# A weight conversion's low-word step moved behind its high-word step, and one accumulator closed by column halves

## The chip, the cores and the metric

The kernel runs on one core of a Trainium2 chip. The metric is the device time of one execution in microseconds (us), lower being better. TensorE (PE in the profile) multiplies matrices into PSUM, VectorE (DVE) and ScalarE (ACT) work element by element, GpSimd (POOL) does small jobs, and SyncE (SP) issues most of the DMA transfers. Each engine works through its own queue of instructions in the order in which they were built, and waits on semaphores for the others.

## The reference

Two computations follow each other. A retention block (batch 4, 8 heads, 768 positions, head width 64) keeps a decaying state per head, and its output becomes a 3072 x 512 matrix x. A feed-forward block then computes `silu(x @ w_in) @ w_out`, with 512 features in and out and 2048 in between:

```
state = gamma * state + outer(k[t], v[t]);   y[t] = scale * q[t] @ state
h = x @ w_in;   g = h / (1 + exp(-h));   out = g @ w_out
```

The five inputs are q, k, v in float32 and the two weight matrices in float64; the output is float32. The kernel receives a float64 weight as two 32-bit words, a low and a high one.

## The kernel before, in words

**Tiling.** The 768 positions are cut into six chunks c of 128, and with the four batches b that makes 24 units of attention. The inner width of 2048 is cut into 16 slices f of 128. For each chunk, x is a block of 512 columns (four batches of 128 positions).

**First stage.** For every pair (c, f) a group of twelve 128x512 matmuls (`multiply`, L682) makes h: eight into the accumulator `ha`, four into `hb`, because each operand is split into a high and a low part to keep float32 accuracy. There are 96 groups. `close_steps` then ends a group: ACT copies `ha` out of PSUM (L692), DVE subtracts `hb` (L697), ACT applies silu (L702), and SP stores the result g to DRAM (L708). The accumulators come from `turn`, which hands out three PSUM banks in rotation, so that the `hb` of a group takes the bank that the `ha` of the group before it had. The attention units are woven between the groups by `visit`.

**Weight conversion.** `load_w` loads a weight slice i (0 to 15 are w_in, 16 to 31 are w_out) as a tile `wf` of 128 x 1024 words into one of two buffers. `convert_steps` turns it into float32: ACT takes the absolute value of the high word (L204, tile `ca`), DVE takes the sign (L207), ACT converts the low word (L210; for w_out in place in `wf`, for w_in into `cw`), DVE clamps, shifts and combines (L212, L216), and DVE adds the low part (L222). A converted w_out slice is stored to DRAM (`wod`) and read back later.

**What sets the order.** PE's order is written by hand. On the other engines it is written by hand up to about the first tenth of the run (`early_order`, ended at L914); after that a scheduler in the build places each instruction by its own estimate of when its inputs are there. `queue(ins)` puts what is built inside it behind the instruction `ins` on that engine's queue; while the order is written by hand (`written`), it does nothing. The high-word step L204 stands inside such a block, the low-word step L210 in none.

**Second stage.** For every chunk, `oa` and `ob` accumulate `g @ w_out` for four batches over 16 slices (L1023). In the last chunk the last two slices are done batch by batch (L1031), first `ob`, then `oa`, so that the batches close one after the other. Each block then goes through ACT (copy `ob`, L1044), DVE (combine with `oa`, L1049) and SP (store, L1052); for the last batch DVE and the store work in two halves of 256 columns.

Of the kernel before, what the change touches and what calls it, by code (L numbers as in the profile page):

```python
# [13 lines left out]
FP32 = mybir.dt.float32  # L14
# [3 lines left out]
AF = mybir.ActivationFunctionType  # L18
# [15 lines left out]
def kernel(  # L34
# [28 lines left out]
    nc = tc.nc  # L63
    B, H, S, D = q.shape
    DM, DF = moe_w_in.shape
    C = 128
# [3 lines left out]
    NF = DF // 128  # L70
# [5 lines left out]
    scale = 1.0 / math.sqrt(D)  # L76
# [24 lines left out]
    def bits(x):  # L101
        return float(np.array(x, np.uint32).view(np.float32))
# [89 lines left out]
    def convert_steps(i, out):  # L192

        t = staged.pop(i)
        if not wide:
            out.append(t)
            return
        words = t.rearrange("p (c w) -> p c w", w=2)
        lo, hi = words[:, :, 0], words[:, :, 1]
        a = conv.tile([128, DM], U32, tag="ca", name=f"ca_{i}")  # L200
        s = conv.tile([128, DM], U32, tag="cs", name=f"cs_{i}")
        r = lo if i >= NF else conv.tile([128, DM], U32, tag="cw", name=f"cw_{i}")
        with queue(evac[0] if evac else None):
            nc.scalar.activation(out=a.bitcast(FP32), in_=hi.bitcast(FP32), func=AF.Abs,  # L204
                                 scale=2.0 ** -3)
        yield
        nc.vector.tensor_scalar(out=s, in0=hi, scalar1=0x80000000, scalar2=None,  # L207
                                op0=ALU.bitwise_and)
        yield
        nc.scalar.activation(out=r.bitcast(FP32), in_=lo, func=AF.Copy, scale=2.0 ** -27,  # L210
                             bias=2.0 ** 25)
        nc.vector.tensor_scalar(out=a.bitcast(FP32), in0=a.bitcast(FP32),  # L212
                                scalar1=bits(872 << 20), scalar2=bits((1127 << 20) - 1),
                                op0=ALU.max, op1=ALU.min)
        yield
        nc.vector.scalar_tensor_tensor(out=s, in0=a, scalar=3, in1=s,  # L216
                                       op0=ALU.logical_shift_left, op1=ALU.bitwise_xor)
        yield
        yield
        yield  # L220
        w = s if i < NF else conv.tile([128, DM], U32, tag="cw", name=f"cw_{i}")
        nc.vector.tensor_tensor(out=w, in0=s, in1=r, op=ALU.add)  # L222
        out.append(w.bitcast(FP32))

    def convert_w(i):

        if patient[0]:
            waiting.append(i + W_AHEAD)
        elif i + W_AHEAD not in staged:
            load_w(i + W_AHEAD)  # L230
        out = []
        steps = convert_steps(i, out)
        for _ in range(6):
            next(steps, None)

        def rounded():
            list(steps)
            return out[0]

        return rounded  # L240

    def early_slice(i):

        out = []
        yield from convert_steps(i, out)
        yield
        steps = split_steps(i, out[0], "wi", scale, w_sb, None)
        next(steps)
        yield from steps
# [4 lines left out]
    def queue(ins):  # L254

        return ExitStack() if written[0] or ins is None else tc.issue_after(ins)
# [69 lines left out]
    for j in range(2):  # L326
        for a in range(HP):
            nc.scalar.activation(out=decay[:, j, a, :], in_=lag[:, :D], func=AF.Exp,
                                 scale=float(lg[2 * a + j]))
# [10 lines left out]
    for h in range(H):  # L340
        nc.scalar.activation(out=gk[:, 0, h : h + 1], in_=pos, func=AF.Exp,
                             scale=float(-lg[h]))
# [27 lines left out]
    def banks(tag, name, n=2):  # L370
        return ps_u.tile([128, n, 512], FP32, tag=tag, name=name)
# [3 lines left out]
    def turn(name):  # L375
        turns[0] += 1
        return ps_h.tile([128, 512], FP32, tag=f"h{turns[0] % 3}", name=name)
# [334 lines left out]
    got, ready, wo, w_got = {}, {}, {}, {}  # L712
# [19 lines left out]
    def w_out(f):  # L732
        list(split_w(f, w_got.pop(f), "wo", 1.0, wo))
        get_w(f + W_READ)
# [3 lines left out]
    def split(n):  # L738
        if n >= len(order):
            return  # L740
        c, f = order[n]
        get(n + G_AHEAD)
        g = got.pop(n)
        if f % 4 == 0:
            blocks[n // 4] = xpool.tile([128, 3, 4, NT], FP32R, tag="xt", name=f"gs_{c}_{f}")
        t = blocks[n // 4][:, :, f % 4, :]
        nc.scalar.activation(out=t[:, 0, :], in_=g, func=AF.Copy, scale=HALF)  # L747
        high = t[:, 0, :].bitcast(FP32)
        nc.vector.tensor_tensor(out=t[:, 1, :], in0=g, in1=high, op=ALU.subtract)  # L749
        nc.vector.scalar_tensor_tensor(out=t[:, 2, :], in0=t[:, 1, :].bitcast(FP32),  # L750
                                       scalar=-1.0 / EPS, in1=high,
                                       op0=ALU.mult, op1=ALU.add)
        ready[n] = t
# [196 lines left out]
    parts = {first_far: FAR}  # L950
# [50 lines left out]
    for c in range(NC):  # L1001
        acc = []
        for b in range(B):
            if b < 2:
                u = banks("sy"[b], f"o{b}_{c}")
                acc.append([u[:, i] for i in range(2)])
            else:
                acc.append([turn(f"oa{b}_{c}"), turn(f"ob{b}_{c}") if b == 2 else
                            banks("q", f"ob{b}_{c}", 1)[:, 0]])
        early_f = NF if c < NC - 1 else NF - 2  # L1010
        for f in range(NF):
            n = c * NF + f
            split(n + S_AHEAD)
            if n < 4:
                w_out(NF - 4 + n)
            t = ready[n]
            if f >= early_f:
                continue
            for b in range(B):
                gh, glo, gm = (t[:, i, ts(b, C)] for i in range(3))  # L1020
                oa, ob = acc[b]
                for o, g, i in (oa, gh, 0), (oa, glo, 1), (ob, gm, 2):
                    nc.tensor.matmul(o, lhsT=g, rhs=wo[f][:, i, :], start=f == 0 and i != 1,  # L1023
                                     stop=f == NF - 1 and i != 0)

        for b in range(B if early_f < NF else 0):
            oa, ob = acc[b]
            for o, parts in (ob, (2,)), (oa, (0, 1)):
                for f in range(early_f, NF):
                    for i in parts:  # L1030
                        nc.tensor.matmul(o, lhsT=ready[c * NF + f][:, i, ts(b, C)],  # L1031
                                         rhs=wo[f][:, i, :], start=False,
                                         stop=f == NF - 1 and i != 0)
        for b in range(B):
            oa, ob = acc[b]
            o = one.tile([128, DM], FP32, tag=("kt", "qt")[b % 2], name=f"o_{c}_{b}",
                         bufs=(2, 3)[b % 2])
            rows = ds(b * S + c * C, C)
            if c < NC - 1:
                nc.scalar.activation(out=o, in_=oa, func=AF.Copy, scale=ONE_E)  # L1040
                nc.vector.tensor_tensor(out=o, in0=o, in1=ob, op=ALU.subtract)  # L1041
                nc.scalar.dma_start(out=out[rows, :], in_=o)
                continue
            nc.scalar.copy(out=o, in_=ob)  # L1044

            n = 2 if b == B - 1 else 1
            for i in range(n):
                cols = ts(i, DM // n)
                nc.vector.scalar_tensor_tensor(out=o[:, cols], in0=oa[:, cols], scalar=ONE_E,  # L1049
                                               in1=o[:, cols], op0=ALU.mult,  # L1050
                                               op1=ALU.subtract)
                nc.sync.dma_start(out=out[rows, cols], in_=o[:, cols])  # L1052
# [30 lines left out]
```

## Time and profile before

| what | us |
|---|---|
| three runs | 625.62, 621.43, 625.50 |
| median | 625.50 |
| the profiled execution, its own time | 627.48 |
| its span, first to last instruction | 625.70 |
| PE matmul busy | 602.2 |
| DVE busy | 393.4 |
| ACT busy | 332.5 |

The profiled execution took 1.78 us more than its span, and 1.98 us more than the median. The first stage ends at about 360 us in the profile, the second fills the rest. A row of the timeline gives the start, the duration, the engine, the line, the operation and its tiles, the number of merged instructions, and in brackets how long the engine was idle before it and what ended that. A row of the waits gives the total, the number of times, and the longest.

### The profile page before, as it was taken

What the parts mean: (1) busy time and instruction counts of PE and PEld (TensorE: products, weight loads), DVE (VectorE), ACT (ScalarE), POOL (GpSimd) and SP (SyncE); (2) the same over time, 40 slices, a digit from 0 to 9 for tenths busy, and PEclk for the clock granted to TensorE, in tenths of its full rate; (3) what the DMA queues carried; (4) which work ended last, traced back from release to release, by engine and by line L of the source; (5) the groups of instructions that cost most, each with busy time, mean ns of one, the idle gap of its engine ahead of it and who ended that gap; (6) DMA issues with size and microseconds to landing.
All of it is one profiled execution on the core that took longest, in us unless ns stands there. A gap on an engine that the chain in (4) does not pass through costs nothing.

```text
span 625.7 us, 13466 instructions
## 1 busy us (share of the span) xinstructions
PE 602.2 (96%) x5384; PEld 494.4 (79%) x5384; DVE 393.4 (63%) x667; ACT 332.5 (53%) x633; POOL 27.9 (4%) x85
## 2 busy tenths in 40 slices
PE   5798999999999899989999999999999999999997
PEld 4677788888787688878787888888888888888886
DVE  4788788678686557765499593553635544554631
ACT  7677998678675567767588651312312221412311
POOL 3000000100031111111000000000000000000000
PEclk9899999999999899999999999999999999999999
DMA  9998876586699589999769443342533423342301
GB/s 191 224 222 186 235 205 205 165 247 202 236 193 203 155 247 235 273 249 287 252 229 310 160 128 101 121 149 69 170 99 103 167 83 119 136 134 77 126 1 67
DMA packets 144335, 108.88 MB, mean 174 GB/s; under 512 B 101137, under 2 KB 109585, under 8 KB 144273
## 3 DMA queue, kind: packets, MB, share of 16 engines
q1 hardware_dynamic: 141392, 102.79, 59.6%
q10 hardware_dynamic: 2880, 5.24, 2.3%
q8 instruction: 42, 0.69, 0.5%
q14 instruction: 21, 0.16, 0.1%
HBM read 66.06 MB, written 36.70 MB: 164 GB/s over the span
## 4 chain that ended last, share of the span: by engine, by line
PE 91%; DMA 3%; SPq 2%; issue 1%; ACT 1%; DVE 1%; DVEq 0%; POOL 0%; POOLq 0%; ACTq 0%
PE ha L682 27%; PE o L1023 20%; PE oa L1023 14%; PE hb L682 14%; PE ob L1023 7%; PE y L529 4%; DMA wf<-in_moe_w_out_dram 2%; PE sc L480 2%; PE sc L490 1%; DMA kqv<-in_q_dram 1%; SPq L165 1%; DMA vf<-in_v_dram 1%; PE kp L454 1%; PE qp L454 1%; SPq L430 0%
## 5 line engine op out<-in xcount | busy, mean ns | idle before, releaser
L682 PE MATMUL ha<-xt,wi 128*128 128x512 f32 x768 | 195.8, 397 | 0.4 <-ACT xt L585 0.4
L682 PEld LDWEIGHTS ha<-xt,wi 128*128 128x128 f32 x768 | 143.9, 190 | 32.5 <-DVE g L697 0.7
L1023 PE MATMUL o<-wo,gs 128*128 128x512 f32 x564 | 143.1, 389 | 0.0
L747 ACT ACTIVATE gs<-gr 128x512 fp32r<-128x512 f32 x96 | 53.7, 621 | 134.1 <-issue 131.8
L1023 PEld LDWEIGHTS o<-wo,gs 128*128 128x128 f32 x564 | 105.9, 188 | 21.8
L749 DVE TENSOR_TENSOR gs<-gr,gs 128x512 fp32r<-128x512 f32 x96 | 62.2, 687 | 90.2 <-ACT gs L747 90.2
L1023 PE MATMUL oa<-wo,gs 128*128 128x512 f32 x376 | 115.9, 389 | 0.0
L697 DVE TENSOR_TENSOR g<-g,hb 128x512 f32<-128x512 f32 x96 | 65.8, 685 | 73.7 <-ACT g L692 54.3
L682 PE MATMUL hb<-xt,wi 128*128 128x512 f32 x384 | 104.3, 394 | 6.3 <-ACT g L692 6.3
L682 PEld LDWEIGHTS hb<-xt,wi 128*128 128x128 f32 x384 | 72.5, 190 | 23.0 <-ACT g L692 7.9
L1023 PEld LDWEIGHTS oa<-wo,gs 128*128 128x128 f32 x376 | 70.6, 188 | 14.7
L702 ACT ACTIVATE g<-g 128x512 f32<-128x512 f32 x96 | 60.4, 629 | 33.0 <-DVE g L697 32.9
L1023 PE MATMUL ob<-wo,gs 128*128 128x512 f32 x188 | 73.7, 392 | 0.0
L692 ACT ACTIVATE g<-ha 128x512 f32<-128x512 f32 x96 | 56.9, 592 | 16.6 <-PE ha L682 14.5
L750 DVE SCALAR_TENSOR_TENSOR gs<-gs 128x512 fp32r<-128x512 f32 x96 | 62.2, 686 | 0.0
L1023 PEld LDWEIGHTS ob<-wo,gs 128*128 128x128 f32 x188 | 35.3, 188 | 8.7 <-DVE o L1041 1.6
L498 DVE TENSOR_TENSOR am<-sc,decay 128x512 f32<-128x512 f32 x24 | 16.6, 690 | 12.8 <-PE sc L490 12.8
L204 ACT ACTIVATE ca<-wf 128x512 f32<-128x512 f32 x32 | 21.5, 672 | 5.0 <-DVE cs L216 2.6
L210 ACT ACTIVATE wf<-wf 128x512 f32<-128x512 uint32 x16 | 10.6, 665 | 25.2 <-DMA wf<-in_moe_w_out_dram 25.2
L1040 ACT ACTIVATE o<-o 128x512 f32<-128x512 f32 x10 | 6.0, 600 | 33.4 <-PE o L1023 33.0
L216 DVE SCALAR_TENSOR_TENSOR cs<-ca,cs 128x512 uint32<-128x512 uint32 x32 | 22.1, 692 | 0.9
L529 PE MATMUL y<-qt,mid 64*64 64x64 f32 x384 | 20.0, 222 | 2.1 <-issue 1.5
(105 smaller groups left out, 564.4 us busy)
## 6 DMA issues: line engine op xcount, KB each, us to landing
gd<-g SPq DMA_DIRECT2D x96, 256.0 KB, 3.4
gr<-gd SPq DMA_DIRECT2D x96, 256.0 KB, 2.7
wf<-in_moe_w_out_dram SPq DMA_DIRECT2D x16, 512.0 KB, 5.0
out_dram<-o ACTq DMA_DIRECT2D x20, 256.0 KB, 2.1
wf<-in_moe_w_in_dram SPq DMA_DIRECT2D x16, 256.0 KB, 4.0
wf<-in_moe_w_in_dram SPq DMA_DIRECT2D x32, 128.0 KB, 3.8
kf<-in_k_dram SPq DMA_DIRECT2D x16, 256.0 KB, 4.1
qf<-in_q_dram SPq DMA_DIRECT2D x16, 256.0 KB, 4.3
```

What stands on the lines that cost most here:

```text
L204: nc.scalar.activation(out=a.bitcast(FP32), in_=hi.bitcast(FP32), func=AF.Abs, scale=2.0 ** -3)
L216: nc.vector.scalar_tensor_tensor(out=s, in0=a, scalar=3, in1=s, op0=ALU.logical_shift_left, op1=ALU.bitwise_xor)
L498: mask = nc.vector.tensor_tensor(out=am[n], in0=sc, in1=decay, op=ALU.mult).ins
L529: i = nc.tensor.matmul(yp[ts(e, D), o, a, :], lhsT=lhsT, rhs=rhs, start=(e, o) not in started, stop=True, skip_group_check=True).ins
L682: nc.tensor.matmul(hb if i == 2 else ha, lhsT=w_sb[f][:, i, ts(kk, 128)], rhs=xt[c][:, i, kk, :], start=kk == 0 and i != 1, stop=kk == KIN ...
L692: copied[:] = [nc.scalar.activation(out=hs, in_=ha, func=AF.Copy, scale=ONE_E).ins]
L697: taken_out[:] = [nc.vector.tensor_tensor(out=hs, in0=hs, in1=hb, op=ALU.subtract).ins]
L702: nc.scalar.activation(out=hs, in_=hs, func=AF.Silu)
L747: nc.scalar.activation(out=t[:, 0, :], in_=g, func=AF.Copy, scale=HALF)
L749: nc.vector.tensor_tensor(out=t[:, 1, :], in0=g, in1=high, op=ALU.subtract)
L750: nc.vector.scalar_tensor_tensor(out=t[:, 2, :], in0=t[:, 1, :].bitcast(FP32), scalar=-1.0 / EPS, in1=high, op0=ALU.mult, op1=ALU.add)
L1023: nc.tensor.matmul(o, lhsT=g, rhs=wo[f][:, i, :], start=f == 0 and i != 1, stop=f == NF - 1 and i != 0)
```

## The change

There are two edits. In `convert_steps` the high-word instruction is kept as `top`, and the low-word instruction is built inside `queue(top)`, which makes it stand behind the high-word one on ACT's queue. In the second stage, the closing matmuls of `oa` for the last batch are cut into two sets of columns: first the four matmuls of the left 256 columns, then the four of the right 256, each with the same stationary operands. Since the lines shift, the low-word step is L211 in the changed kernel, the closing matmuls L1038, the DVE step after them L1057 and the store L1060.

```diff
         with queue(evac[0] if evac else None):
-            nc.scalar.activation(out=a.bitcast(FP32), in_=hi.bitcast(FP32), func=AF.Abs,
-                                 scale=2.0 ** -3)
+            top = nc.scalar.activation(out=a.bitcast(FP32), in_=hi.bitcast(FP32), func=AF.Abs,
+                                       scale=2.0 ** -3).ins
...
-        nc.scalar.activation(out=r.bitcast(FP32), in_=lo, func=AF.Copy, scale=2.0 ** -27,
-                             bias=2.0 ** 25)
+        with queue(top):
+            nc.scalar.activation(out=r.bitcast(FP32), in_=lo, func=AF.Copy, scale=2.0 ** -27,
+                                 bias=2.0 ** 25)
...
-            for o, parts in (ob, (2,)), (oa, (0, 1)):
+            ends = [(ob, (2,), slice(None))]
+            if b < B - 1:
+                ends.append((oa, (0, 1), slice(None)))
+            else:
+                ends += [(oa, (0, 1), slice(i * DM // 2, (i + 1) * DM // 2))
+                         for i in range(2)]
+            for o, parts, cols in ends:
                 for f in range(early_f, NF):
                     for i in parts:
-                        nc.tensor.matmul(o, lhsT=ready[c * NF + f][:, i, ts(b, C)],
-                                         rhs=wo[f][:, i, :], start=False,
-                                         stop=f == NF - 1 and i != 0)
+                        nc.tensor.matmul(o[:, cols], lhsT=ready[c * NF + f][:, i, ts(b, C)],
+                                         rhs=wo[f][:, i, cols], start=False,
+                                         stop=f == NF - 1 and i != 0,
+                                         skip_group_check=cols.start == DM // 2)
```

## The prediction

> **What bounds the kernel.** I read the shares of the chain that ended last first: PE holds 91% of it, so a change counts by what it does to PE's gaps. Then the waits, for ACT as the engine the first edit touches and for PE as the one that counts.
>
> ```profile
> PE 91%; DMA 3%; SPq 2%; issue 1%; ACT 1%; DVE 1%; DVEq 0%; POOL 0%; POOLq 0%; ACTq 0%
> ```
>
> ```profile
> ACT wf L210 <- DMA wf<-in_moe_w_out_dram: 25.2, 12, 6.4
> ...
> PE hb L682 <- ACT g L692: 6.3, 3, 4.4
> ...
> ACT ca L204 <- DMA wf<-in_moe_w_out_dram: 2.2, 2, 1.3
> ```
>
> ACT stood 25.2 us, 12 times, in front of the low-word step until the slice's load had landed, because the scheduler had put L210 a whole conversion ahead of its L204. PE paid for it three times, 6.3 us in all: an `hb` group could not start, since the bank still held an `ha` whose copy (L692) was queued behind the waiting L210. The timeline shows the worst place (ACT rows, then PE rows, then granted clock by stretch, PEclk):
>
> ```profile
> 198.21 0.58 ACT L585 ACTIVATE xt<-y 128x512 fp32r<-128x512 f32 x1
> 205.23 0.65 ACT L210 ACTIVATE wf<-wf 128x512 f32<-128x512 uint32 x1 [6.44 <-DMA wf<-in_moe_w_out_dram]
> 205.79 0.58 ACT L692 ACTIVATE g<-ha 128x512 f32<-128x512 f32 x1
> 206.27 1.33 ACT L437 COPY qt<-qw 128x1024 uint16<-128x1024 uint16 x1
> 207.47 1.33 ACT L437 COPY kt<-kw 128x1024 uint16<-128x1024 uint16 x1
> 208.66 0.63 ACT L702 ACTIVATE g<-g 128x512 f32<-128x512 f32 x1
> ```
>
> ```profile
> 206.42 2.02 PE L682 MATMUL hb<-xt,wi 128*128 128x512 f32 x4 [4.40 <-ACT g L692]
> 208.24 2.78 PE L682 MATMUL ha<-xt,wi 128*128 128x512 f32 x8
> 210.86 1.07 PE L682 MATMUL hb<-xt,wi 128*128 128x512 f32 x4
> ```
>
> ```profile
> 206.50:211.00 4.50, 4.50 (x13) 3.56 (x14) 3.07 (x5) 3.75 (x5) 0.00 (x0) 0.62 0.19 71
> 211.00:250.00 39.00, 39.00 (x528) 32.34 (x527) 26.17 (x46) 24.79 (x42) 6.33 (x9) 1.00 0.88 222
> ```
>
> ACT is stuck for 6.44 us, PE for 4.40 of them, and afterwards PE runs at a granted clock of 0.62 before it is back at 1.00.
>
> **Edit one: what moves.** In the built program the orders of PE, DVE, POOL and SP are unchanged but for the tail, and no DMA is issued in another order. On ACT, 15 of the 32 low-word steps move: one of w_in (it ran at 82.0 us, and goes behind its L204 at 91.7) and 14 of w_out. L210 of slices 21 and 25 stood behind its L204 before. The work is the same: 0.66 us each.
>
> *What goes, place by place.* An undisturbed group takes 2.72 us (starts of its four `hb` and eight `ha` matmuls 0.91 and 1.81 us apart).
> - At 206.42: 4.40 us idle. From that `hb` to the next, 210.86 - 206.42 = 4.44 us instead of 2.72: 1.72 more by the clock. Sum 6.12.
> - At 275.67: 1.73 us idle, and 0.15 in the next group (278.54 - 275.67 = 2.87). Sum 1.88.
> - At 170.94: 0.18 us idle, and 0.15 until the attention matmuls that follow (1.15 after the `hb` start, 1.00 at an undisturbed place). Sum 0.33.
>
> Together 8.33 us. The other nine waits cost PE nothing, and their removal gives nothing: an `ha` copy may start 2.72 - 0.59 = 2.13 us after its matmuls end before the next `hb` is held up, and some waits fell beside attention matmuls.
>
> *What is late next.* The load's wait now falls on L204, and the copies, silus and joins behind L204 on ACT would wait with it. In the trace L204 ran 2.6 us (165.57 against a landing by 162.97) to 28 us after the L210 of its slice had ended its wait, so it should wait for nothing there. The two L204s that did wait (1.34 us at 229.61, 0.87 at 269.93) had no PE gap behind them; they stay. At the worst place the next waiter is the join of `kw` (L437), whose transpose was issued at 195.72 and held SP for 3.61 us until 199.33. No row shows its landing; other transposes landed 1.9 to 3.4 us after their issue ended, so here 201.2 to 202.7. The join (1.33), silu (0.6) and the next `ha` copy (0.6) then end at 203.7 to 205.2, and PE wants that bank at about 204.6: between 0 and 0.6 us lost. I take 0.3.
>
> *What the added order costs.* L211 stands 0.57 us ahead of the silu (L702) that used to come there, and silu releases the store of g on SP and the loads behind it. The slack of 2.13 us covers it; DVE needs the low part only at L222, after L212 and L216, 1.1 us of work behind L204, so the pair is done first. Without that cover it would be 0.57 us each, which is a rival below.
>
> **Edit two.** Rows of the tail:
>
> ```profile
> 620.84 1.07 PE L1031 MATMUL oa<-wo,gs 128*128 128x512 f32 x4
> 621.04 0.59 ACT L1044 COPY o<-ob 128x512 f32<-128x512 f32 x1 [0.74 <-PE ob L1031]
> 622.00 0.76 DVE L1049 SCALAR_TENSOR_TENSOR o<-oa,o 128x256 f32<-128x256 f32 x2 [0.67 <-PE oa L1031]
> ```
>
> DVE's two halves begin 0.09 us after the last matmul. What the edit could bring is that the left half (0.42 us) begins while PE still works on the right: at most 0.34 us. But in the built program the left half waits for the count of the eighth matmul, so nothing overlaps. What remains is eight matmuls for four. No row has 256 columns. The nearest: 128 columns, four transposes of L454 from 86.23 to the next tile's first at 86.66, 0.108 us apart; 512 columns, 0.227 us apart. Eight cost 0.86 to 1.81 us against 0.91 now: -0.04 to +0.91. On the line between the rows (nearer to 128 columns) one takes 0.148 us, eight 1.18: I take +0.28, all of it on the path, since nothing comes after.
>
> The Trainium skill speaks against this edit: "PSUM — Partial Sum Buffer", in "PSUM bank collisions raise a hardware error", says that PSUM is to be guarded by bank and quadrant and not by address, because an engine reading other columns of the bank that TensorE writes still collides. By that rule the halves of one bank cannot overlap at all; without it the edit would gain up to 0.34 us less the extra matmul time. No run here shows a collision.
>
> **The sum.** -8.33 + 0.30 + 0.28 = -7.75 us. Against the profiled execution: span 625.70 to 617.95, own time 627.48 to 619.73. The median shown is 1.98 us below that own time. If those 1.98 us have nothing to do with the stalls, the median goes to 617.75; if the median run merely stalled less, it ends near 619.7. I forecast 618.5.
>
> **Rivals.**
> - *The wait is handed on.* If the `kw` transpose lands only when the weight load did (205.2), its join, a silu and the next copy end at 207.8, and PE waits 3.2 us at 204.6, with the low clock (1.7) again: 4.9 us come back in place of the 0.3, about 622.4. For it: no landing is recorded there, and DMA was 94% busy from 200 to 206.5. Against it: other transposes landed within 5.8 us of the start of their issue.
> - *The stalls of the profile are larger than those of the usual run.* The three runs differ by 4.2 us, half of what I remove. If the usual run had only 4 us of it: 621.5. For it: the fastest run. Against it: two of three runs lie at 625.5.
> - *Slower: L204 becomes the waiter.* The scheduler chose L204's place by its estimate; if the loads are later than L204, the 8.33 us of stalls stay, and each of 16 w_out slices puts one L211 (0.66) more between the landing and the next `ha` copy: 16 x 0.66 = 10.6, so 636. It decides once L204 starts before the landing by more than the 2.13 us of slack. Against it: 2.6 us or more to spare in the trace, and neither L204 that waited cost PE anything.
> - *The change doesn't do what it says* is true of edit two, and in the sum.
>
> **How the numbers follow.** The forecast has 0.72, wait handed on 0.12, smaller stalls 0.10, slower 0.06. One per cent of 625.5 is 6.25 us, about what a measurement of this kernel can tell from no change; the mark is 619.25. The forecast lies close to it: I give 0.62 of its 0.72 to below the mark, 0.10 to above. So faster 0.62, within 1% 0.32 (0.10 + 0.12 + 0.10), slower 0.06. The range goes down to 614.5: the fastest run shown less 8.33 us is 613.1, the median less 8.33 and 0.04 is 617.1, and I go two thirds of the way. It goes up to 623.0, which takes in the first two rivals and the forecast with the dearest matmuls (+0.63).
>
> **What would show it.** Right: the waits no longer name the low-word step; `hb` waits for L692 under 0.7 us in all; the granted clock is 1.00 from 200 to 215 us; the second stage begins about 8 us earlier. Edit two: the DVE's left half starts after the eighth matmul, and the eight start about 0.15 us apart. Wrong: ACT idle in front of L204 for more than the present 2.2 us, or in front of L437; PE gaps at other groups; or a kernel before that stalls by other amounts in its other runs.

## The result, and the profile after

| | median, us | runs | ratio to before, 95% interval |
|---|---|---|---|
| before | 623.14 | 6 | |
| changed | 617.72 | 6 | 0.9901 [0.9874, 0.9929] |
| before, on a later occasion | 622.55 | 26 | |
| changed, on a later occasion | 617.71 | 12 | 0.9925 [0.9898, 0.9953] |

The change makes the kernel faster by 0.7% to 1.0%, some 5 to 6 us. The forecast was 618.5. The gain lies at the one per cent mark, on neither side of it beyond doubt: the first ratio makes it 0.99%, the later one 0.75%. The median lies below the 619.25 that the prediction had set as the mark, but the kernel before came out lower as well, so the chance of 0.62 that it put on a gain of more than one per cent is not borne out.

The profiled execution of the changed kernel has a span of 616.1 us, 9.6 less than the one of before; that is more than the medians differ, and the sections below say why. First the shares of the chain, from the page:

```profile
PE 86%; ACT 5%; DMA 4%; SPq 3%; DVE 1%; issue 1%; DVEq 0%; POOL 0%; POOLq 0%; ACTq 0%
```

PE still carries the chain. Its share fell from 91%, and ACT's rose from 1% to 5%: in this execution more of the chain runs through the work that feeds PE. PE itself is busy 598.7 us, 97% of the span.

Then the waits of the changed kernel (total in us, number of times, longest):

```profile
ACT g L693 <- DMA gd<-g: 8.9, 9, 2.2
...
ACT ca L204 <- DMA wf<-in_moe_w_out_dram: 3.1, 2, 2.7
...
PE hb L683 <- ACT g L693: 1.1, 2, 0.9
...
ACT kt L438 <- DMA kw<-kp: 0.7, 1, 0.7
```

The 25.2 us in front of the low-word step are gone: no row names it (L211 now). L204, which took over the wait for the load, waits 3.1 us in place of 2.2. PE's wait for an `ha` copy fell from 6.3 to 1.1 us. Two waits have come up that were small or absent before: the copy itself (L693) waits for stores of g to land, 8.9 us in place of 1.0, and the join of `kw` (L438) waits once.

The place that cost most before, on ACT, and the one row of PE there that has a wait:

```profile
196.28 0.57 ACT L586 ACTIVATE xt<-y 128x512 fp32r<-128x512 f32 x1
197.20 0.60 ACT L693 ACTIVATE g<-ha 128x512 f32<-128x512 f32 x1 [0.35 <-ACT xt L586]
197.70 1.35 ACT L438 COPY qt<-qw 128x1024 uint16<-128x1024 uint16 x1
199.71 1.36 ACT L438 COPY kt<-kw 128x1024 uint16<-128x1024 uint16 x1 [0.67 <-DMA kw<-kp]
200.93 0.62 ACT L703 ACTIVATE g<-g 128x512 f32<-128x512 f32 x1
201.46 0.58 ACT L693 ACTIVATE g<-ha 128x512 f32<-128x512 f32 x1
202.79 0.63 ACT L703 ACTIVATE g<-g 128x512 f32<-128x512 f32 x1 [0.76 <-DVE g L698]
205.51 0.60 ACT L693 ACTIVATE g<-ha 128x512 f32<-128x512 f32 x1 [2.08 <-DMA gd<-g]
```

```profile
206.16 1.21 PE L683 MATMUL hb<-xt,wi 128*128 128x512 f32 x4 [0.89 <-ACT g L693]
```

Between L586 and the copy that follows it lies nothing of the kind of the 6.44 us of before. Two groups later the third buffer of g is not free, since its store has not landed, and PE loses 0.89 us. The granted clock (the third figure from the end of a row of the stretches) stays at full speed:

```profile
200.00:215.00 15.00, 14.12 (x181) 11.37 (x180) 8.90 (x16) 8.63 (x14) 2.43 (x3) 1.00 0.74 207
```

The tail of the changed kernel:

```profile
611.17 1.11 PE L1038 MATMUL oa<-wo,gs 128*128 128x256 f32 x8
611.38 0.59 ACT L1052 COPY o<-ob 128x512 f32<-128x512 f32 x1 [0.74 <-PE ob L1038]
612.38 0.75 DVE L1057 SCALAR_TENSOR_TENSOR o<-oa,o 128x256 f32<-128x256 f32 x2 [0.71 <-PE oa L1038]
```

DVE begins after the last of the eight matmuls, 1.21 us after the first of them started; before, it was 1.16 us after the first of four. The left half overlaps with nothing.

**Where the time went.** PE's and DVE's orders are the same in both kernels, so the 96 subtractions of `hb` (L697, L698) can be laid side by side. The lead of the changed execution over the one of before, in us:

| stretch of before's profile | lead won in it |
|---|---|
| up to 161 us | 1.70 |
| 161 to 180 (slice 19) | 0.48 |
| 180 to 220 (slice 20) | 5.10 |
| 220 to 263 | 0.00 |
| 263 to 296 (slice 26) | 2.02 |
| 296 to 360 | 0.39 |
| second stage and tail | -0.09 |

Between 161 and 360 us the two executions differ by 7.99 us. The first 1.70 us are won ahead of every low-word step that PE had waited behind: 3.09 us before the first group's subtraction, of which 1.39 are given back by 97 us. Edit one is not their cause, since the execution of edit two alone, below, also wins 3.10 us there and has 1.75 left at 161 us. Nor do the last 0.39 us look like its work: in the same stretch, edit two alone wins 0.48 us and a second execution of the unchanged kernel 0.50.

### The profile page after: what moved, and what is told of

Same layout as the page of the kernel before. It is cut to its first block, busy times and chain, and to the rows that moved or that the text cites. A ratio compares the mean times of both kernels' runs of the same rounds, so it can differ in the third digit from the quotient of the medians.

```text
span 616.1 us, 13482 instructions
## 1 busy us (share of the span) xinstructions
PE 598.7 (97%) x5388; PEld 491.9 (80%) x5388; DVE 391.2 (64%) x667; ACT 332.0 (54%) x633; POOL 28.4 (5%) x85
## 4 chain that ended last, share of the span: by engine, by line
PE 86%; ACT 5%; DMA 4%; SPq 3%; DVE 1%; issue 1%; DVEq 0%; POOL 0%; POOLq 0%; ACTq 0%
PE ha L683 25%; PE o L1024 21%; PE oa L1024 14%; PE hb L683 13%; PE ob L1024 7%; PE y L530 3%; DMA gd<-g 2%; SPq L165 2%; PE sc L481 1%; PE sc L491 1%; ACT g L693 1%; ACT kf L399 1%; DMA kqv<-in_q_dram 1%; PE o L1038 0%; SPq L187 0%
## 5 line engine op out<-in xcount | busy, mean ns | idle before, releaser
L683 PE MATMUL ha<-xt,wi 128*128 128x512 f32 x768 | 193.2, 393 | 0.7 <-ACT xt L586 0.7
L683 PEld LDWEIGHTS ha<-xt,wi 128*128 128x128 f32 x768 | 142.0, 188 | 32.1 <-ACT xt L586 1.2
L698 DVE TENSOR_TENSOR g<-g,hb 128x512 f32<-128x512 f32 x96 | 65.7, 684 | 68.4 <-ACT g L693 42.8
L693 ACT ACTIVATE g<-ha 128x512 f32<-128x512 f32 x96 | 56.9, 592 | 30.3 <-PE ha L683 16.1
L204 ACT ACTIVATE ca<-wf 128x512 f32<-128x512 f32 x32 | 21.5, 672 | 5.9 <-DMA wf<-in_moe_w_out_dram 3.1
L1048 ACT ACTIVATE o<-o 128x512 f32<-128x512 f32 x10 | 6.0, 598 | 33.4 <-PE o L1024 33.0
L592 DVE SCALAR_TENSOR_TENSOR xt<-xt 128x512 fp32r<-128x512 f32 x28 | 19.1, 689 | 0.6
```

What stands on the lines that cost most here:

```text
L204: top = nc.scalar.activation(out=a.bitcast(FP32), in_=hi.bitcast(FP32), func=AF.Abs, scale=2.0 ** -3).ins
L592: nc.vector.scalar_tensor_tensor(out=x[2], in0=x[1].bitcast(FP32), scalar=-1.0 / EPS, in1=x[0].bitcast(FP32), op0=ALU.mult, op1=ALU.add)
L683: nc.tensor.matmul(hb if i == 2 else ha, lhsT=w_sb[f][:, i, ts(kk, 128)], rhs=xt[c][:, i, kk, :], start=kk == 0 and i != 1, stop=kk == KIN ...
L693: copied[:] = [nc.scalar.activation(out=hs, in_=ha, func=AF.Copy, scale=ONE_E).ins]
L698: taken_out[:] = [nc.vector.tensor_tensor(out=hs, in0=hs, in1=hb, op=ALU.subtract).ins]
```

## The experiments

**Each edit by itself.** The first kernel has the `queue(top)` of edit one and the closing loop of before; the second has the closing loop of the change and the low-word step of before.

> Edit one without the tail edit. My theory (three waits of the low-word step cost PE about 8 us, the tail edit nothing but eight shorter matmuls): the same as the changed kernel within 0.3 us, 0.9% to 1.3% below before, and in the profile the time from the last L1031 matmul's start row to DVE's first half is 0.05 us shorter than in the changed kernel (1.16 instead of 1.21 us). The rival that the tail edit brings part of the gain (its DVE half overlapping) expects 0.3 us more than the changed kernel.

> The tail edit without edit one. My theory: the same as before, +0.05 us in the profile's tail (DVE's left half starts 1.21 us after the first of the eight matmuls, not 1.16), the 25 us of ACT's waits for the weight loads in front of the low-word step still there, and PE's wait of 4 to 6 us. Rival (overlap works): 0.3 us faster, DVE's left half starting before the last matmul.

Measured: edit one alone 618.04 us, ratio 0.9915 [0.9885, 0.9945]; edit two alone 623.65 us, ratio 1.0006 [0.9975, 1.0036]. The tail of edit one alone gives DVE's start 1.16 us after the first matmul (611.20, 612.36), that of edit two alone 1.21:

```profile
615.03 1.11 PE L1037 MATMUL oa<-wo,gs 128*128 128x256 f32 x8
616.24 0.76 DVE L1056 SCALAR_TENSOR_TENSOR o<-oa,o 128x256 f32<-128x256 f32 x2 [0.71 <-PE oa L1037]
```

So the whole gain is edit one's, and edit two costs 0.05 us, which no timing here could show. The waits of edit two alone are those of before, though not their size:

```profile
ACT wf L210 <- DMA wf<-in_moe_w_out_dram: 22.0, 10, 3.8
PE hb L682 <- ACT g L692: 3.9, 3, 1.8
```

In this execution of the same order PE lost 3.9 us instead of 6.3.

**Which of the moved steps count.** Edit one for three slices alone, and for all the others alone, without edit two:

```diff
-        with queue(top):
+        with queue(top if i in (19, 20, 26) else None):        # three_slices
+        with queue(top if i not in (19, 20, 26) else None):    # all_but_three
```

> Edit one for weight slices 19, 20 and 26 alone (the three whose low-word step PE waited behind), no tail edit; the other low-word steps stay where the scheduler had put them. My theory: all of the gain, 0.9% to 1.3% below before, with some 16 us of ACT's waits for loads left in the profile and PE's waits for L692's copy under 1.5 us. Rival (the gain comes from the ACT waits in general, 25 us spread over twelve places): about a third of the gain, 0.3% to 0.4%.

> The complement: edit one for all slices but 19, 20 and 26, no tail edit. My theory: the same as before within 0.3%, PE's wait of 4 to 5 us behind slice 20's low-word step still there with the low clock after it, and 1 to 3 us at slice 26. Rival (waits in general): two thirds of the gain, 0.6% to 0.8%.

Measured: three slices 617.96 us, ratio 0.9927 [0.9897, 0.9956]; all others 623.65 us, ratio 1.0006 [0.9972, 1.0040]. The waits of the two, the three slices first:

```profile
ACT wf L211 <- DMA wf<-in_moe_w_out_dram: 12.4, 6, 2.7
...
PE hb L683 <- ACT g L693: 1.8, 2, 1.5
```

```profile
ACT wf L211 <- DMA wf<-in_moe_w_out_dram: 10.1, 3, 5.8
PE hb L683 <- ACT g L693: 5.0, 3, 3.8
```

The first kernel has 12.4 us of ACT's waits left and nearly the whole gain. The second has only three waits left, 10.1 us, and no gain. What counts is what an engine's wait holds up, not how long it is in all: twelve of the fifteen moved steps are worth nothing. The expected 16 us and under 1.5 us came out as 12.4 and 1.8. Most of that 1.8 us is a milder case of the rival "the wait is handed on": in this execution the join of `kw` (L438) waited 2.7 us for its transpose, and the copy behind it held PE up for 1.5 us.

**How far the stall varies.** The kernel before, unchanged, profiled once more:

> The kernel before, unchanged, for a second profile of it. If the spread of its runs (618.7 to 630.0 us) comes from the wait for slice 20's load, a faster execution shows PE idle there for under 2 us and no low clock after it, a slower one 4 us or more with the low clock. Rival (the spread comes from the head of the run, before 60 us): the same stall of 4.4 us and other times before the first group.

Measured: 623.92 us, span 622.2. It falls between the two ends that were expected:

```profile
202.78 1.39 PE L682 MATMUL hb<-xt,wi 128*128 128x512 f32 x4 [3.39 <-ACT g L692]
203.97 3.43 PE L682 MATMUL ha<-xt,wi 128*128 128x512 f32 x8
...
272.64 1.20 PE L682 MATMUL hb<-xt,wi 128*128 128x512 f32 x4 [2.28 <-ACT g L692]
```

Four executions so far have the early low-word step of slice 20. PE's rows there, of edit two alone and of all others alone:

```profile
201.75 1.20 PE L682 MATMUL hb<-xt,wi 128*128 128x512 f32 x4 [1.77 <-ACT g L692]
```

```profile
204.65 2.07 PE L683 MATMUL hb<-xt,wi 128*128 128x512 f32 x4 [3.76 <-ACT g L693]
206.52 3.62 PE L683 MATMUL ha<-xt,wi 128*128 128x512 f32 x8
```

After an idle of 1.77 us, and of 2.28 us at slice 26, the four matmuls take 1.20 us; after 3.39, 3.76 and 4.40 us the twelve that follow, or some of them, run slowly. So the stall at slice 20 is 1.8 to 4.4 us long. After the three longer ones a second cost comes on top: the group that begins there takes 4.46, 5.28 and 4.44 us from its `hb` to the next, in place of 2.72, which is 1.7 to 2.6 us more, and after the idle of 3.76 us the next group loses another 0.35. Between the groups on either side of the place (196.95 and 219.72 us in before) the execution of edit two alone is 3.5 us shorter than that of before. The Trainium skill has a rule that fits: "TensorE: Matmul & The Clock Gate", in "Part 1: The HAM clock gate (the "warmup" mystery)", says that the clock falls to half after an idle window of about 3.4 us. The rows agree as far as they reach, with no drop after 2.28 us of idle and one after 3.39. The stretches of all others alone show a granted clock of 0.50 from 205 to 209 us; the low clock there begins at 203.75 us, 2.9 us after PE's last matmul ended, so the figure is not a sharp limit in this trace.

What makes the length vary is the landing of slice 20's load. Counted from the start of the last subtraction before the stall (196.95 us in before), it landed after 8.26 us (before), 7.26 (before again), 5.64 (edit two alone) and 7.63 (all others alone), and in all four the stall is 3.9 us less. Two things move the landing: the transpose of `kw`, which stands ahead of the load in SP's queue and held SP for 3.61, 2.04, 1.88 and 3.12 us, and the time from the load's issue to its landing, 5.2, 5.9, 4.9 and 5.2 us.

The rival of that expectation holds in part as well: not the same stall, but other times before the first group. In the stretch from 20 to 34 us, where the orders of all kernels are the same, the granted clock differs from execution to execution. Before, changed, and edit one for w_out alone (below):

```profile
20.00:34.00 14.00, 10.84 (x209) 9.07 (x209) 8.31 (x16) 7.30 (x16) 0.18 (x2) 0.76 1.02 217
```

```profile
20.00:34.00 14.00, 10.84 (x274) 8.84 (x273) 10.99 (x21) 9.61 (x20) 0.26 (x3) 1.00 0.97 206
```

```profile
20.00:34.00 14.00, 11.57 (x182) 9.70 (x181) 8.96 (x17) 8.43 (x18) 0.18 (x2) 0.63 0.93 207
```

The first group's subtraction starts at 33.4, 30.3 and 34.6 us in the three. The head alone thus makes executions differ by 4 us, and the 1.70 us of the table above are what is left of such a difference.

**The moved step of w_in.** The changed profile has a gap of 0.25 us in front of `hb` at 92.23 us, with slice 6's L211 on ACT a little ahead of the copy that PE waited for. Edit one for w_out alone, no edit two:

```diff
-        with queue(top):
+        with queue(top if i >= NF else None):
```

> Edit one for the 16 w_out slices alone, no tail edit: w_in slice 6 keeps its early low-word step. Theory A (the moved step of slice 6 put 0.57 us ahead of an eviction and cost the changed kernel up to 1.1 us at 92 us of its profile): 0.3 to 1 us below edit one alone, no gap of hb near 92 us. Theory B (that gap came from a late store of g at 84 us in that one execution; the kernel with edit one alone shows none): the same as edit one alone within 0.3 us.

Measured: 618.00 us, ratio 0.9925 [0.9897, 0.9953], against 0.9915 for edit one alone on another occasion. Theory A is not borne out in the time: leaving slice 6 where it was brings nothing that can be measured. The subtractions show why. In the changed kernel, edit one alone and all others alone, which move this step, the lead over before rises by 0.57 us at the subtraction at 83 us of before and falls by 0.56 or 0.57 (in the changed profile by 1.12) at the one at 94 us; the kernels that leave it show neither. The move gains at one place what it loses at the next.

**The next wait.** A fourth buffer for the tile of g, paid for with one buffer of the state and one of `mid`; the order of instructions stays the same. Once on top of the kernel just told of, run on two occasions, and once on the kernel before:

```diff
-    hpool = pool("hpool", 3)
+    hpool = pool("hpool", 4)
...
-        mid = one.tile([128, HP, D], FP32, tag="mid", name=f"mid_{n}", bufs=2)
+        mid = one.tile([128, HP, D], FP32, tag="mid", name=f"mid_{n}", bufs=1)
...
-            state[b] = one.tile([128, HP, D], FP32, tag="state", name=f"state_{n}", bufs=B + 2)
+            state[b] = one.tile([128, HP, D], FP32, tag="state", name=f"state_{n}", bufs=B + 1)
```

> As the run with edit one for w_out alone, with a fourth buffer for the tile of g (hpool), paid for by one state buffer and one mid buffer less; the order of the instructions is the same on every engine. Theory: what is left of PE's wait near slice 20 (0.6 to 0.9 us) comes from ACT's copy waiting for the store of g (7 to 9 us of such waits in all); they go, PE's wait for L693 there goes to zero, 0.5 to 1 us faster than with three buffers. Rival (the join of kw behind its late transpose holds the copy): the waits for the stores go and PE's wait stays, no change in time.

> The version with edit one for w_out alone and a fourth buffer for g, again, beside the changed kernel on one chip. Expected: 1.0 to 1.6 us below the changed kernel (the waits for stores of g in front of ACT's copy gone, 0.9 us of PE's wait with them).

> The changed kernel again, on the same chip: 0.8% to 1.2% below before, and a PE wait of 0 to 1 us near 205 us behind the store of g.

> The kernel before with the fourth buffer for g alone (one state and one mid buffer less), the low-word step where it was. If the low-word step's wait comes first, the fourth buffer alone brings nothing: the same as before within 0.3%, PE's wait of 2 to 5 us at slice 20 still there. Rival (stores of g are a cost of their own): 0.2% to 0.4% faster by itself.

| kernel | us | ratio to before |
|---|---|---|
| fourth buffer and edit one for w_out | 616.43 | 0.9894 [0.9855, 0.9933] |
| the same again | 616.48 | 0.9904 [0.9871, 0.9937] |
| changed kernel, beside the second | 617.71 | 0.9925 [0.9898, 0.9953] |
| fourth buffer alone | 626.61 | 1.0055 [1.0019, 1.0091] |

In the second profile with four buffers the waits for stores are down to one of 0.4 us, and no `hb` waits for a copy:

```profile
ACT g L693 <- DMA gd<-g: 0.4, 1, 0.4
```

This version has the lowest medians of all that ran, 1.2 us below the changed kernel on the same chip. The two intervals overlap, so it is the best candidate, not a proven winner over the changed kernel. Nor do the profiles show that the fourth buffer took a wait off PE. The kernel with three buffers that it was built on has 4.0 us of waits for stores in front of the copy, and none of its `hb` groups waits for a copy either; between 180 and 220 us of before, that kernel and both profiles with four buffers win the same 6.28 us over before. So the size of the gain is near what was expected, but the cause named for it is not confirmed; with one profile of the one and two of the other, where the lower median comes from stays open.

The fourth buffer alone makes the kernel slower, which neither theory had expected. Its profile shows the stall of slice 20 at its longest:

```profile
ACT wf L210 <- DMA wf<-in_moe_w_out_dram: 22.8, 9, 7.6
...
PE hb L682 <- ACT g L692: 7.0, 2, 5.5
```

```profile
207.45 2.08 PE L682 MATMUL hb<-xt,wi 128*128 128x512 f32 x4 [5.50 <-ACT g L692]
```

The load took 6.6 us from issue to landing here, 4.9 to 5.9 in the four profiles above with three buffers. Why it takes longer with a fourth buffer stays open; one profile cannot say whether it always does.

**The pace of short matmuls.** The last accumulator closed in four sets of 128 columns (`slice(i * DM // 4, (i + 1) * DM // 4)` for `i in range(4)`):

> The changed kernel with the last accumulator closed in four sets of 128 columns, 16 matmuls in place of 8. If a matmul's pace is its columns plus a constant (256 columns took 0.12 us against 0.227 for 512), 128 columns take about 0.07 us and the tail grows by 0.1 us; if a floor near 0.108 us (the pace of L455's transposes) binds, 16 take 1.73 us and DVE starts 0.75 us later than in the changed kernel, 1.95 us after the first of them.

```profile
610.55 1.90 PE L1038 MATMUL oa<-wo,gs 128*128 128x128 f32 x16
612.54 0.76 DVE L1057 SCALAR_TENSOR_TENSOR o<-oa,o 128x256 f32<-128x256 f32 x2 [1.50 <-PE oa L1038]
```

A single run took 618.00 us. DVE starts 1.99 us after the first of sixteen. With 0.227 us for each of four 512-column matmuls and a start 1.16 us after the first, some 0.25 us is not pace; what is left gives (1.21 - 0.25) / 8 = 0.120 us at 256 columns and (1.99 - 0.25) / 16 = 0.109 at 128. The floor theory is right: the transposes that the prediction used, at 0.108 us, have 128 columns too. The Trainium skill, in "TensorE: Matmul & The Clock Gate", "LDWEIGHTS (loading the stationary operand)", gives columns over 1.2 in nanoseconds for loading the stationary operand, 107 ns for the 128 here, which the measured 0.109 fits. That the loading is what sets the floor is not shown: no run here changes it alone.

## Why the prediction was right, point by point

- **What bounds.** Right. ACT's wait in front of the low-word step reached PE through the queue, the `ha` copy and the bank. The two complementary kernels show it: three slices carry the gain, the others none.
- **What goes, place by place.** The sum of 8.33 us less 0.30 for the next waiter, 8.03, came out as 7.99 between 161 and 360 us of the two profiles. Slice 19 gave 0.48 for 0.33, slice 26 2.02 for 1.88, the rest of the stage 0.39 for nothing, and slice 20 5.10 for 5.82. That the sum fits so closely is in part luck, since the 0.39 does not look like the edit's.
- **The size for the usual run.** Too large. The first ratio makes the gain 6.2 us (0.0099 of 623.14), the later one 4.7, not 7.75; the medians differ by 5.4 and 4.8. The term that was mis-sized most is slice 20's 6.12 us, read from one execution. Measured against edit one for w_out alone, where no `hb` waited, the four executions with the early step lost 6.28 (before), 5.33, 2.79 and 6.84 us between 180 and 220 us of before, 5.3 on average. The other term is the 0.30 for what is late next: the same measure gives 1.2 and 0.7 us in the two profiles of the changed kernel and 0.9 in that of edit one alone. With 5.3 and 0.9 in their places, and 0.05 for edit two, the sum is about 6.6 us, an estimate from these few profiles. The rival of the smaller usual stall had the direction right, with too small a gain (4 us). That the forecast came within 0.8 us is in part luck, a cancellation: with more runs the median of before was lower too, 623.14 for 625.50, by about as much as the gain had been oversized.
- **What is late next.** The join of `kw` did wait, 0.67 us, and held up no group of PE by itself. That a store of g would hold the copy, for 2.08 us, was not foreseen: the prediction followed ACT's queue and the PSUM banks, but not the three buffers of g. The loss of 0.89 us stands in place of the 0.3 taken. In the kernel with three slices alone the join did reach PE, for 1.5 us, so the rival "the wait is handed on" was a real one, with half of the 3.2 us that it named.
- **L204 as the waiter, and the pair's cost.** Right that neither matters: 3.1 us of waits, none with a gap of PE behind it, and the moved w_in step is worth nothing that can be measured.
- **Edit two.** Right in mechanism: no overlap, only dearer matmuls. The size of +0.28 was wrong, 0.05 measured. The failed step is the line drawn between the rows of 128 and 512 columns. The three paces (0.109, 0.120 and 0.227 us) fit the larger of two terms, a floor near 0.109 us and one that follows the columns, with the second just above the first at 256 columns; three points can't show more. Whether the two halves of one bank could overlap was not tried, because that would need the wait itself taken away.
- **What would show it.** The second stage begins 9.69 us earlier (359.71, now 350.02), more than the 8 us expected, 1.70 of it won before the first of these waits. PE's `hb` waits for the copy came to 1.1 us, above the 0.7 us set as the sign, and the eight matmuls start 0.12 us apart, not 0.15. All the signs of being wrong came up in a small form: ACT waited 3.1 us in front of L204, above the 2.2, and 0.7 us in front of the join of `kw`, neither with a gap of PE directly behind it; PE had gaps at other groups, of 0.89 and 0.25 us; and the kernel before does stall by other amounts in its other runs, which is the main reason why the gain came out smaller.

## What to carry to other kernels

A step that waits for a transfer blocks everything behind it in its engine's queue, so a scheduler that hoists it ahead of a copy out of PSUM can stop TensorE although the step itself is not urgent; put it where its data is surely there. Price a wait by what it delays on the bounding engine: here 25 us of waits were worth 6, and three of fifteen moves were worth all of it. Where a stall is ended by a DMA, read its length from more than one execution before putting it in a sum.

## What was not expected of the hardware

Granted clock between 20 and 34 us varied between 0.63 and 1.00 from one execution to another with the same instructions, and the first group came up to 4.3 us later where it was low (30.3 to 34.6). One DMA transpose held SP's queue for 1.88 us (edit two alone) to 3.88 us (edit one alone) at the same place of the same SP order, where the median of the ten transposes of `kw` before is 1.36 us. A fourth buffer for g, with which the kernel has its lowest median when edit one is in place, made it 0.2% to 0.9% slower without edit one.
